# Storing rounded weight quarters at once, moving the GpSimd sums behind the last weight piece, reordering a piece's rounding steps, and turning one attention tile on TensorE

## The chip, the cores and the metric

The kernel runs on one core of a Trainium2 chip. The metric is device time in microseconds (us) of one execution, lower is better. A core has TensorE (PE, matrix products), VectorE (DVE), ScalarE (ACT) and GpSimd (POOL), and a queue on SyncE (SP) that here issues nearly all DMA transfers. [...]

## The reference

A local attention is followed by a Fourier mix and a two-layer network with a ReLU:

```python
q_c = q.reshape(B, H, nc, chunk, D)            # B=8, H=8, S=576, D=64, chunk=64
scores = 1/sqrt(D) * matmul(q_c, k_c.transpose)
attn = softmax(scores)                         # within each chunk of 64 tokens
x = matmul(attn, v_c)  -> (8, 576, 512)
u = x + real(fft(fft(x, axis=1), axis=2))
un = (u - mean) / sqrt(var + 1e-6)             # over the 512 features
out = u + maximum(un @ w_ch1, 0) @ w_ch2       # w_ch1 512 x 2048, w_ch2 2048 x 512
```

q, k, v are float32. The two weight matrices arrive as float64, so the kernel rounds them to float32 itself, with integer operations on the two 32-bit words of each number.

## The kernel before

**Groups and steps.** Tokens are cut into tiles of 128 rows, three kinds of them: LO and HI (low and mirrored high chunks of one batch) and RE (the middle chunks of two batches). For each of the eight batches there is a group of four tiles (LO and HI), and a ninth group holds the four RE tiles. The main loop runs the network (`mlp`, L1234) group after group. Each `yield` of it is one step `t`. Group 0 has 16 steps up (`up_first`, L1044, one weight piece each) and 16 steps down (`down_plain`, L1088, one row block `m` of `w_ch2` each); a step is eight matmul records of 128x512 here[...]. From group 1 on the down product, and from group 2 on the up product, use a Strassen-Winograd form with seven products in place of eight (`up_halves` L1124, `down_halves` L1168). It needs sums of weight quarters; these are computed once, put into HBM (`s1`, `s2`) and fetched again as slabs.

**What is interleaved.** While group g is multiplied, the attention and the Fourier mix of batch g+1 run as a generator (`side`, L1289), a due share per step. Attention of a tile has four parts: `att_T` turns q and k, `att_S` scores (tile `sc`), `att_P` turns the exponentials, `att_V` multiplies by v (tile `xp`). From the third batch on (`n >= first[2]`) `att_T` is a DVE block transpose (L366) on a special load layout (L203, 8 DMAs for q and 8 for k); before that it is four PE transposes each and an ACT copy (L374 to L387). The third batch begins with tile 9, an RE tile, and its `att_T` falls into step 15 of group 0. The Fourier mix (`fourier`, L742) is: products into `z` (L669), ACT copies (L694, L708), three DVE operations (`z_joined`, L696), ACT copies into `zr` and `zf`, products into `mix` (L788), sums, mean and variance, then normalising (`normed` L929) and turning (`turned` L947) into the next group's `unT`.

**Rounding the weights.** There are 32 pieces of 128x512: 16 of `w_ch1`, then 16 of `w_ch2`, landing in seven raw buffers: two in `yall`, five in `xall`. Pieces from `N_LAST` = 26 on use three of the buffers only. `round_weight(i)` (L301) does the head of piece i and the tail of piece i-1: DVE masks the fraction (L322) and the exponent (L325), ACT converts the fraction (L314) and the exponent in two steps (L317, L320); then DVE adds the low word (L335), merges the sign (L336) and multiplies (L337). L336 is the last to read the raw buffer, after which the next piece is loaded (L299). `round_next` is called once or twice a step, except in a step where `side` reports a heavy part.

**Sums for the second matrix.** `keep2(i)` (L1006), i = 0 to 3, makes four sums on GpSimd (L1017) from quarters of `w2`, in `yall` for even i and in `xall` for odd i, and then queues seven stores on SP: three plain quarters and four sums (L1021). The loop takes five parts of it as soon as more than 26 pieces have been begun, the rest behind the last piece. `keep1` (L989) does the like for the first matrix in group 1, and uses `yall` for even i.

**ReLU.** At steps 4, 8, 12 and 16, ACT applies the ReLU to four PSUM tiles (L1065), which frees those PSUM buffers for PE's next products. In ACT's order these come behind the three ACT parts of the piece that was begun in the step before.

Of the kernel before, what the change touches and what calls it, by code (L numbers as in the profile page):

```python
# [8 lines left out]
FP32 = mybir.dt.float32  # L9
U32 = mybir.dt.uint32  # L10
# [6 lines left out]
def kernel(  # L17
# [32 lines left out]
    nc = tc.nc  # L50
# [130 lines left out]
    def load(n, which="qk"):  # L181

        for src, dst, nm, eng in ((q, qs, "q", nc.sync), (k, ks, "k", nc.scalar if n == 0 else nc.sync)):
            if nm not in which:
                continue
            if n == first[1] and nm == "q":
                one_p.tile([128, 96], FP32, tag="pad_c", name="pad_c")  # L190
            if n < first[1]:
                i = 2 * n + (nm == "k")
                t = start[:, (4 + i) * DM:(5 + i) * DM].rearrange("p (j r d) -> p j (r d)", r=2, d=D)
            else:
                t = one_p.tile([128, NJ, 4 * D], FP32, tag=nm, name=nm)
            if n >= first[2]:
                (b0, c0), (b1, c1) = chunks(n)
                parts = [(0, 32, b0, min(c0, c1))] if b0 == b1 else [(0, 16, b0, c0), (16, 16, b1, c1)]
                for g in range(4):
                    e, x0 = g // 2, g % 2 * 32  # L200
                    for r0, rows, b, c in parts:
                        from_ = src[b, e:H:2, c * CH:c * CH + 4 * rows, :].rearrange("j (p t) d -> p j (t d)", t=4)
                        eng.dma_start(  # L203
                            out=t[32 * g + r0:32 * g + r0 + rows, :, 0:4 * D - 32],
                            in_=from_[:, :, x0:x0 + 4 * D - 32],
                        )
                dst[n] = t
                continue
            t = t.rearrange("p j (r d) -> p (j r) d", d=D)[:, 0:H]
            (b0, c0), (b1, c1) = chunks(n)  # L210
            if b0 == b1 and c1 == c0 + 1:
                parts = [(0, 128, b0, c0)]
            else:
                parts = [(0, CH, b0, c0), (CH, CH, b1, c1)]
            for p0, np_, b, c in parts:
                eng.dma_start(
                    out=t[p0:p0 + np_], in_=src[b, :, c * CH:c * CH + np_, :].rearrange("h p d -> p h d")
                )
            dst[n] = t
# [70 lines left out]
    def raw(i):  # L290
        return spaces[raws[i]].bitcast(U32).rearrange("p (f r) -> p f r", r=2)
# [9 lines left out]
    def round_weight(i, later=None, parts="ht"):  # L301

        if "h" in parts and i < len(pieces):
            w, t = pieces[i][0], raw(i)
            lo, hi, wi = t[:, :, 0], t[:, :, 1], w.bitcast(U32)  # L310
            p = power[i] = three_p.tile([128, 512], U32, tag="o", name="power")

            def fraction(w=w, wi=wi):
                nc.scalar.activation(out=w, in_=wi, func=ACTF.Copy, scale=2.0 ** -20, bias=1.0)  # L314

            def exponent(p=p):
                nc.scalar.activation(out=p, in_=p, func=ACTF.Relu, scale=-1.0, bias=top[:, 0:1])  # L317

            def power_(p=p):
                nc.scalar.activation(out=p, in_=p, func=ACTF.Relu, scale=-8.0, bias=top[:, 1:2])  # L320

            nc.vector.tensor_scalar(wi, hi, 0x000FFFFF, None, ALU.bitwise_and)  # L322
            if later is None:
                fraction()
            nc.vector.tensor_scalar(p, hi, 0x7FF00000, None, ALU.bitwise_and)  # L325
            if later is None:
                exponent()
                power_()
            else:
                later += [fraction, exponent, power_]  # L330
        if "t" in parts and 0 < i <= len(pieces):
            w, t = pieces[i - 1][0], raw(i - 1)
            lo, hi = t[:, :, 0], t[:, :, 1]
            p = power.pop(i - 1)
            nc.vector.scalar_tensor_tensor(w, lo, 2.0 ** -52, w, ALU.mult, ALU.add)  # L335
            nc.vector.scalar_tensor_tensor(p, hi, 0x80000000, p, ALU.bitwise_and, ALU.bitwise_or)  # L336
            nc.vector.tensor_tensor(out=w, in0=w, in1=p.bitcast(FP32), op=ALU.mult)  # L337
            r = raws.pop(i - 1)
            if i - 1 + len(spaces) < N_EARLY or r < N_LATE:
                free.append(r)  # L340
            load_weight(max(raws, default=i - 1) + 1)
# [9 lines left out]
    def att_T(n, which="qk"):  # L351

        if n >= first[2]:
            for src, dst, nm in ((qs, qT, "qT"), (ks, kT, "kT")):
                if nm[0] not in which:
                    continue
                a = src.pop(n).rearrange("p j (t b d) -> p j t b d", t=4, b=2)[:, :, :, 0]  # L360
                t = one_p.tile([128, NJ, 2, CH + 1], FP32, tag=nm, name=nm)
                low = kind(n) == LO and nm == "qT"
                to = t[:, :, :, CH:0:-1] if low else t[:, :, :, 0:CH]
                if kind(n) == HI:
                    to = to[:, :, ::-1]
                nc.vector.transpose(out=to.rearrange("p j c (r t) -> p j t c r", t=4), in_=a)  # L366
                if low:
                    nc.gpsimd.tensor_copy(t[:, :, :, 0:1], t[:, :, :, CH:CH + 1])
                dst[n] = t.rearrange("p j c t -> p (j c) t")
            if n + 1 < NT:  # L370
                load(n + 1, which)
            return
        a = qs.pop(n)
        pt = turn(lambda j: a[:, 2 * j:2 * j + 2, :].rearrange("p h d -> p (h d)"))  # L374
        t = one_p.tile([128, 2 * NJ, CH + 1], FP32, tag="qT", name="qT")
        low = kind(n) == LO
        nc.scalar.copy(t[:, :, CH:0:-1] if low else t[:, :, 0:CH], pt.rearrange("p j (c t) -> p (j c) t", c=2))
        if low and n < first[1]:
            nc.scalar.copy(t[:, :, 0:1], t[:, :, CH:CH + 1])
        elif low:  # L380
# [625 lines left out]
    def keep2(i):  # L1006

        m = 2 * i
        b11, b12 = w2[:, m:m + 2, 0:HM], w2[:, m:m + 2, HM:DM]
        b21, b22 = w2[:, HF + m:HF + m + 2, 0:HM], w2[:, HF + m:HF + m + 2, HM:DM]  # L1010
        to = xall[:, 2 * G:2 * G + 4, 0:DM] if i % 2 else yall
        o1, o2, o3, o4 = (to[:, j].rearrange("p (m e) -> p m e", m=2) for j in range(4))
        for out_, in0, in1, op in (
            (o1, b12, b11, ALU.subtract), (o2, b22, o1, ALU.subtract),
            (o3, b22, b12, ALU.subtract), (o4, b21, o2, ALU.subtract),
        ):
            nc.gpsimd.tensor_tensor(out=out_, in0=in0, in1=in1, op=op)  # L1017
            yield
        to = s2.rearrange("o p (m e) -> o p m e", m=HF)
        for o, a in enumerate((b11, o2, o1, o3, b21, b22, o4)):  # L1020
            nc.sync.dma_start(out=to[o, :, m:m + 2], in_=a)  # L1021
        yield

    first_of = {1: 2, 2: 1}
    n_slab = {1: 0, 2: 0}
# [214 lines left out]
    with tc.manual_schedule():  # L1240
# [61 lines left out]
        for g in range(NG):  # L1302
            begin.append(begin[-1] + (KF if g < first_of[1] else 2 * HF) + (KF if g < first_of[2] else 2 * NO))
        ready_at = [begin[g] + (2 * KF - 7 if g < first_of[2] else 2 * HF + 4) for g in range(NG)]
        conv2 = iter([step for i in range(HF // 2) for step in [keep2(i)]])
        conv1 = iter([step for i in range(4) for step in [keep1(i)]])

        def chain(gens):
            for gen in gens:
                yield from gen  # L1310

        n_sum = 0
        conv2, conv1 = chain(conv2), chain(conv1)
        t = 0
        for g in range(NG):
            for _ in mlp(g):
                t += 1
                heavy = False
                if t == 8:
                    nc.scalar.copy(tk, early_tk[:, :, :, 0:NE])  # L1320
                if cur < len(sides):
# [8 lines left out]
                            pass  # L1330
                        cur, done = cur + 1, 0
                if not heavy:
                    round_next()
                    if t <= 2 or t < KF and t % 4 == 0 or t >= KF + 3:
                        round_next()

                for _ in range(3):
                    if n_w > len(pieces) or n_w > N_LAST and n_sum < 5:
                        next(conv2, None)
                        n_sum += 1  # L1340
                if t == begin[1] - 1:
                    for _ in conv2:
                        pass
# [58 lines left out]
```

## Time and profile before

| what | value |
|---|---|
| runs before | 1083.34, 1083.85, 1084.11 us (median 1083.85) |
| the profiled execution's own time | 1083.94 us |
| its span, first to last instruction | 1082.2 us |
| PE busy | 1057.6 us, 98% |
| DVE, ACT, POOL busy | 586.8, 309.4, 328.6 us |
| moved by DMA | 192.65 MB |
| mean granted TensorE clock | 0.995 |

The span is told from its start. Group 0 goes up from about 50 to 115 us and down from 117 to 195 us; group 1 follows. A "wait" line names the engine, the tile that it was about to write, and the instruction whose end released it. A timeline line has the start, the duration, engine, line, operation, output<-inputs and shape; an idle time before it stands in square brackets.

### The profile page before, as it was taken

The numbers are of one execution on the slowest core, as the hardware profiler recorded it, in microseconds if no ns is written. First come the engines' busy times: TensorE is split into PE (matmuls) and PEld (weight loads), VectorE is DVE, ScalarE is ACT, GpSimd is POOL, SyncE is SP. The second block draws the span as 40 slices with busy tenths as digits, with TensorE's granted clock in tenths as the row PEclk, the third lists the DMA queues.
The fourth block names the chain that finished last, engine by engine and source line by source line (L and its number), as shares of the span: only waits on it lengthen the run. The fifth ranks groups of instructions, "written<-read, shape, count | busy, mean of one in ns | idle before, by whom it ended". The sixth has DMA issues, their size and how long they took to land.

```text
span 1082.2 us, 19747 instructions
## 1 busy us (share of the span) xinstructions
PE 1057.6 (98%) x7410; PEld 841.1 (78%) x7410; DVE 586.8 (54%) x1271; ACT 309.4 (29%) x730; POOL 328.6 (30%) x475
## 2 busy tenths in 40 slices
PE   8999989999999999999999999999999999999998
PEld 6645445446888888788888888888888888888887
DVE  4899986325556555664555555735664534323411
ACT  4788463222113320232122311331134103101300
POOL 4301026384513350163215331525151401310140
PEclk9999989999999999999999999999999999999999
DMA  8766555598557635793578356854663355346232
GB/s 176 237 196 180 153 175 199 143 292 275 192 172 229 198 118 173 222 266 105 168 214 252 112 176 179 253 174 150 184 199 104 144 173 177 123 151 213 78 117 78
DMA packets 147948, 192.65 MB, mean 178 GB/s; under 512 B 66284, under 2 KB 104172, under 8 KB 140686
## 3 DMA queue, kind: packets, MB, share of 16 engines
q1 hardware_dynamic: 144204, 187.98, 57.1%
q10 hardware_dynamic: 3330, 2.76, 1.0%
q8 instruction: 59, 0.97, 0.3%
q0 software_dynamic: 320, 0.66, 0.3%
q14 instruction: 35, 0.29, 0.1%
HBM read 167.22 MB, written 24.12 MB: 177 GB/s over the span
## 4 chain that ended last, share of the span: by engine, by line
PE 81%; DVE 6%; DMA 6%; ACT 4%; SPq 2%; issue 1%; POOL 1%; DVEq 0%; ACTq 0%; POOLq 0%
PE pb L1190 21%; PE pa L1141 17%; PE pa L1190 15%; PE pb L1141 13%; PE pt L347 3%; PE up L1074 2%; PE dn L1095 2%; PE mix L788 2%; PE z L669 1%; PE sc L398 1%; PE xp L448 1%; PE up L1054 1%; DMA v<-in_v_dram 1%; DMA out_dram<-o 1%; DMA q<-in_q_dram 1%
## 5 line engine op out<-in xcount | busy, mean ns | idle before, releaser
L1141 PE MATMUL pa<-unT,wa 128*128 128x256 f32 x672 | 159.9, 381 | 2.5 <-DVE wa L1149 2.5
L1141 PEld LDWEIGHTS pa<-unT,wa 128*128 128x128 f32 x672 | 126.3, 190 | 20.3 <-DVE wa L1149 3.0
L1042 POOL TENSOR_TENSOR h<-h 128x256 f32<-128x256 f32 x64 | 55.2, 870 | 232.6 <-DVE wb L1040 140.1
L1190 PE MATMUL pa<-wb,h 128*128 128x256 f32 x512 | 115.7, 380 | 0.0
L1190 PE MATMUL pb<-wb,h 128*128 128x256 f32 x512 | 114.9, 379 | 0.0
L1141 PE MATMUL pb<-wa 128*128 128x256 f32 x448 | 106.6, 381 | 0.0
L1190 PEld LDWEIGHTS pa<-wb,h 128*128 128x128 f32 x512 | 96.1, 190 | 12.9
L1190 PEld LDWEIGHTS pb<-wb,h 128*128 128x128 f32 x512 | 96.3, 190 | 12.6
L1141 PEld LDWEIGHTS pb<-wa 128*128 128x128 f32 x448 | 84.3, 190 | 11.5
L1095 PE MATMUL dn<-wb,h 128*128 128x512 f32 x128 | 60.8, 625 | 2.6 <-ACT h L1065 2.6
L505 POOL COPY xall<-xall 1x512 f32<-1x512 f32 x28 | 17.3, 617 | 149.7 <-DVE xall L465 120.4
L1147 DVE TENSOR_TENSOR wa<-pb,wa 128x256 f32<-128x256 f32 x56 | 23.8, 424 | 69.7 <-ACT wa L1146 69.7
L1190 PE MATMUL pb<-wb,yall 128*128 128x256 f32 x256 | 58.2, 381 | 0.0
L1190 PE MATMUL pb<-wb 128*128 128x256 f32 x256 | 57.7, 379 | 0.0
L1190 PE MATMUL pa<-wb,yall 128*128 128x256 f32 x256 | 57.6, 379 | 0.0
L1074 PE MATMUL up<-unT,wa 128*128 128x512 f32 x128 | 56.8, 596 | 0.0
L1146 ACT COPY wa<-pa 128x256 f32<-128x256 f32 x56 | 20.8, 372 | 123.8 <-PE pa L1141 81.0
L1141 PE MATMUL pa<-wa 128*128 128x256 f32 x224 | 53.9, 383 | 0.0
L1141 PE MATMUL pb<-unT,wa 128*128 128x256 f32 x224 | 53.0, 380 | 0.0
L1190 PEld LDWEIGHTS pa<-wb,yall 128*128 128x128 f32 x256 | 48.0, 190 | 6.1
L1190 PEld LDWEIGHTS pb<-wb,yall 128*128 128x128 f32 x256 | 47.7, 190 | 6.3
L1190 PEld LDWEIGHTS pb<-wb 128*128 128x128 f32 x256 | 47.7, 190 | 5.9
(265 smaller groups left out, 1770.0 us busy)
## 6 DMA issues: line engine op xcount, KB each, us to landing
wb<-s SPq DMA_DIRECT2D x56, 1024.0 KB
wa<-s SPq DMA_DIRECT2D x196, 256.0 KB
xall<-in_moe_w_ch_dram SPq DMA_DIRECT2D x22, 512.0 KB
q<-in_q_dram SPq DMA_DIRECT2D x96, 112.0 KB
k<-in_k_dram SPq DMA_DIRECT2D x96, 112.0 KB
v<-in_v_dram SPq DMA_DIRECT2D x124, 64.0 KB
yall<-in_moe_w_ch_dram SPq DMA_DIRECT2D x10, 512.0 KB
s<-wb SPq DMA_DIRECT2D x20, 256.0 KB
```

What stands on the lines that cost most here:

```text
L347: nc.tensor.transpose(pt[:, j, :], src(j), ident)
L398: nc.tensor.matmul(out=sc[t0:t0 + CH, e, j * CH:(j + 1) * CH], lhsT=a[r0:r0 + D, 2 * j + c, 0:CH], rhs=b[r0:r0 + D, 2 * j + c, 0:CH], star ...
L448: nc.tensor.matmul(out=xp[0][e][t0:t0 + CH, j * DV:(j + 1) * DV], lhsT=a[r0:r0 + CH, j, t0:t0 + CH], rhs=b[r0:r0 + CH, c, j, :], start=Tru ...
L505: nc.gpsimd.tensor_copy(to, from_)
L788: nc.tensor.matmul(out=mix[:, cols], lhsT=zt[:, T], rhs=tab, start=(T == 0), stop=(T == 3), skip_group_check=True,)
L1042: nc.gpsimd.tensor_tensor(out=h1[:, m, hi], in0=h1[:, m, lo], in1=h1[:, m, hi], op=ALU.subtract)
L1074: nc.tensor.matmul(out=up, lhsT=w1[:, kk, m * 128:(m + 1) * 128], rhs=unT[:, kk], start=(kk == 0), stop=(kk == KD - 1),)
L1095: nc.tensor.matmul(out=dn, lhsT=h1[:, m, s * 128:(s + 1) * 128], rhs=w2[:, m, :], start=(m == 0), stop=(m == KF - 1),)
L1141: nc.tensor.matmul(out=dst, lhsT=w[:, kk, r], rhs=rhs[o][:, kk], start=(o in (0, 1) and kk == 0), stop=(kk == 1), skip_group_check=True,)
L1146: nc.scalar.copy(a, dst)
L1147: nc.vector.tensor_tensor(out=b, in0=pbs[r][:, 0], in1=a, op=ALU.add)
L1190: nc.tensor.matmul(out=dst, lhsT=lhs[:, m], rhs=w[:, m], start=(o in (0, 2) and m == 0), stop=(m == HF - 1), skip_group_check=True,)
```

## The change

Four things are altered.

1. `keep2` stores only its four sums. A new `keep2_whole(i)` queues the three plain quarters of `w2` as soon as the pieces that they consist of have been begun and left behind by two more. The sums are all taken behind the last piece, in the order i = 1, 0, 3, 2.
2. In `round_weight` the exponent mask comes first, then two of the three tail operations of the piece before, then the fraction mask, then the tail's product. ACT gets exponent, second exponent step, fraction.
3. In steps 3, 7, 11 and 15 the three ACT parts of the piece are held back (`late`) until the next step's products and ReLUs have been issued.
4. The bounds `n >= first[2]` in `load` and `att_T` become `n > first[2]`: tile 9 is loaded in natural order (two DMAs for q, two for k) and turned by PE and ACT.

```diff
@@ load, att_T
-            if n >= first[2]:
+            if n > first[2]:
@@ round_weight
-        if "h" in parts and i < len(pieces):
+        head, tail = "h" in parts and i < len(pieces), "t" in parts and 0 < i <= len(pieces)
+        if head:
...
-            nc.vector.tensor_scalar(wi, hi, 0x000FFFFF, None, ALU.bitwise_and)
-            if later is None:
-                fraction()
             nc.vector.tensor_scalar(p, hi, 0x7FF00000, None, ALU.bitwise_and)
             if later is None:
                 exponent()
                 power_()
+        if tail:
+            w_, t_ = pieces[i - 1][0], raw(i - 1)
+            p_ = power.pop(i - 1)
+            nc.vector.scalar_tensor_tensor(w_, t_[:, :, 0], 2.0 ** -52, w_, ALU.mult, ALU.add)
+            nc.vector.scalar_tensor_tensor(p_, t_[:, :, 1], 0x80000000, p_, ALU.bitwise_and, ALU.bitwise_or)
+        if head:
+            nc.vector.tensor_scalar(wi, hi, 0x000FFFFF, None, ALU.bitwise_and)
+            if later is None:
+                fraction()
             else:
                 later += [fraction, exponent, power_]
-        if "t" in parts and 0 < i <= len(pieces):
...
-            nc.vector.scalar_tensor_tensor(w, lo, 2.0 ** -52, w, ALU.mult, ALU.add)
-            nc.vector.scalar_tensor_tensor(p, hi, 0x80000000, p, ALU.bitwise_and, ALU.bitwise_or)
-            nc.vector.tensor_tensor(out=w, in0=w, in1=p.bitcast(FP32), op=ALU.mult)
+        if tail:
+            nc.vector.tensor_tensor(out=w_, in0=w_, in1=p_.bitcast(FP32), op=ALU.mult)
@@ keep2
-        for o, a in enumerate((b11, o2, o1, o3, b21, b22, o4)):
+        for o, a in ((1, o2), (2, o1), (3, o3), (6, o4)):
             nc.sync.dma_start(out=to[o, :, m:m + 2], in_=a)
         yield
+
+    def keep2_whole(i):
+        m = 2 * i
+        to = s2.rearrange("o p (m e) -> o p m e", m=HF)
+        for o, m0, e0 in ((0, m, 0), (4, HF + m, 0), (5, HF + m, HM)):
+            nc.sync.dma_start(out=to[o, :, m:m + 2], in_=w2[:, m0:m0 + 2, e0:e0 + HM])
@@ main loop
-        conv2 = iter([step for i in range(HF // 2) for step in [keep2(i)]])
+        conv2 = iter([step for i in range(HF // 2) for step in [keep2(i ^ 1)]])
...
             for _ in mlp(g):
                 t += 1
                 heavy = False
+                for do in late:
+                    do()
+                late = []
...
                 if not heavy:
-                    round_next()
+                    round_next(late if t < KF and t % 4 == 3 else None)
...
-                for _ in range(3):
-                    if n_w > len(pieces) or n_w > N_LAST and n_sum < 5:
+                while n_whole < HF // 2 and n_w > KF + HF + 2 * n_whole + 2:
+                    keep2_whole(n_whole)
+                    n_whole += 1
+                if n_w > len(pieces):
+                    for _ in range(3):
                         next(conv2, None)
-                        n_sum += 1
```

More of the change, by code (lines that the diff above doesn't have):

```diff
@@ L301, in round_weight @@
     def round_weight(i, later=None, parts="ht"):
-        if "h" in parts and i < len(pieces):
+        head, tail = "h" in parts and i < len(pieces), "t" in parts and 0 < i <= len(pieces)
+        if head:
             w, t = pieces[i][0], raw(i)
-            lo, hi, wi = t[:, :, 0], t[:, :, 1], w.bitcast(U32)
+            hi, wi = t[:, :, 1], w.bitcast(U32)
             p = power[i] = three_p.tile([128, 512], U32, tag="o", name="power")
@@ L328, in round_weight @@
                 power_()
+        if tail:
[7 more added lines that the diff above has]
+                fraction()
             else:
                 later += [fraction, exponent, power_]
-        if "t" in parts and 0 < i <= len(pieces):
[L332 to L337, printed above, removed]
+        if tail:
+            nc.vector.tensor_tensor(out=w_, in0=w_, in1=p_.bitcast(FP32), op=ALU.mult)
             r = raws.pop(i - 1)
@@ L351, in att_T @@
     def att_T(n, which="qk"):
-        if n >= first[2]:
+        if n > first[2]:
             for src, dst, nm in ((qs, qT, "qT"), (ks, kT, "kT")):
@@ L1310, in chain @@
                 yield from gen
-        n_sum = 0
+        n_whole, late = 0, []
         conv2, conv1 = chain(conv2), chain(conv1)
```

## The prediction

> **What bounds the kernel now.** I read the page first, then PE's waits, then the granted clock in short windows, and then the timelines of DVE, ACT, SP and POOL around each wait.
>
> ```profile
> PE 1057.6 (98%) x7410; PEld 841.1 (78%) x7410; DVE 586.8 (54%) x1271; ACT 309.4 (29%) x730; POOL 328.6 (30%) x475
> ...
> PE mix L788 <- ACT zr L735: 4.4, 1, 4.4
> PE dn L1095 <- ACT h L1065: 2.6, 1, 2.6
> PE pt L347 <- ACT un L942: 2.1, 3, 1.0
> PE sc L398 <- DVE rd L461: 1.4, 1, 1.4
> PE up L1054 <- ACT h L1065: 1.1, 2, 0.6
> ```
>
> PE sets the time. Only what PE loses can be won, and in the waits that is little: the five lines shown are 11.6 us, and all but 1.6 us of them (two of the `un` waits at 44 us) lie between 64 and 217 us, where the weights are rounded. From 262 us on PE waits 2.5 us in all, and the change does not touch that part. Behind the two longest waits the clock drops too:
>
> ```profile
> 117.00:119.00 2.00, 1.81 (x2) 0.84 (x3) 1.57 (x3) 1.59 (x4) 0.22 (x2) 0.55 1.04 236
> 156.00:158.00 2.00, 1.83 (x6) 1.70 (x7) 1.97 (x5) 1.97 (x9) 0.00 (x0) 0.50 1.06 388
> ```
>
> (Columns: window, length, busy PE, PEld, DVE, ACT, POOL, clock, DMA share, GB/s.) The first down step takes 5.39 us instead of 3.60; after the second wait the `mix` products and a step lose 2.7 us. So the most that can be won is about 0.64 + 0.44 (up) + 2.57 + 1.8 (seam from up to down) + 4.42 + 2.7 (mix) + 0.5 + 1.4 = 14.5 us.
>
> Why is `mix` late? ACT's copies before it stand behind the rounding of piece 29, and DVE is late with that:
>
> ```profile
> 139.61 0.69 DVE L337 TENSOR_TENSOR wb<-wb,power 128x512 f32<-128x512 f32 x1
> 140.66 1.33 DVE L322 TENSOR_SCALAR wb<-xall 128x512 uint32<-128x512 uint32 x1 [0.36 <-DMA xall<-in_moe_w_ch_dram]
> 141.91 1.49 DVE L325 TENSOR_SCALAR power<-xall 128x512 uint32<-128x512 uint32 x1
> 143.33 1.75 DVE L335 SCALAR_TENSOR_TENSOR wb<-xall,wb 128x512 f32<-128x512 uint32 x1
> 145.01 0.68 DVE L336 SCALAR_TENSOR_TENSOR power<-xall,power 128x512 uint32<-128x512 uint32 x1
> ...
> 140.44 1.26 POOL L1017 TENSOR_TENSOR yall<-wb,yall 128x512 f32<-128x512 f32 x1 [10.62 <-DVE wb L337]
> 141.67 1.45 POOL L1017 TENSOR_TENSOR yall<-wb 128x512 f32<-128x512 f32 x1
> 143.08 1.45 POOL L1017 TENSOR_TENSOR yall<-wb,yall 128x512 f32<-128x512 f32 x1
> ```
>
> The three DVE operations beside the three sums take 4.57 us; elsewhere 0.42 + 0.42 + 0.68 = 1.52. The sums cost DVE 3.05 us here, and the first sum, at 128.56, stretches L520 from 0.69 to 1.77: 1.08 more.
>
> **What the Trainium skill says.** "SBUF — State Buffer", section "SBUF: two separate sides": VectorE and GpSimd share one port pair, held as an exclusive lock for a whole instruction. The trace agrees: each of those DVE operations is longer by about one sum. "TensorE: Matmul & The Clock Gate", section "The HAM clock gate": a free-running window of 3413 ns, half clock after an idle one. The records show half clock for 3.41 us from 117.2 and 6.83 us from 154.8, behind idle times of 2.57 and 4.42 us, and none behind 1.43 us. [...]here a 512 KB piece issued at 137.00 ends a wait at 140.66, 3.6 us.
>
> **The change part by part.** The profiled execution's span is 1082.2 of its own 1083.94 us, so 1.7 us lie outside; its time is 0.1 above the median. I subtract from the median.
>
> *Held-back ACT parts.* At steps 4 and 12 the ReLUs no longer wait for 1.9 us of rounding on ACT: 0.64 + 0.44 = 1.08 won. Hidden cost: the piece's ACT parts come after four ReLUs (2.0 us), and DVE's next piece waits for them.
>
> *New step order.* DVE keeps five operations, 2.60 us a piece (heads at 132.41, 135.02, 137.62). But the fraction leaves DVE at 0.34 + 0.60 + 0.60 + 0.34 = 1.88 and ACT at 2.5 us into a piece, and is needed at 2.94; before, the most urgent ACT result had 1.5 us of slack. Wherever ACT has the q and k copies (0.95) or ReLUs in between, DVE waits. Going through the ACT queue from 47 to 112 us I find waits of 0.7 at the start, and about 1.3 (step 4), 1.0 (step 8) and 1.6 (step 12), part of it caught up where DVE waited for PE before (0.83 at 79.8); two old waits of 0.67 go. I take DVE as 2.0 us later at 112 us; bounds 0 and 3.5. This is covered while DVE leads PE: at 90.8 it begins piece 16, which PE needs at 117.
>
> *Tile 9 on PE.* DVE loses two transposes (1.09 + 1.08, at 112.34 and 113.28): 2.2 won, which offsets the 2.0. PE gains eight transposes, 0.87 us by the other tiles' records; ACT two copies, 0.95. Of SP's 16 DMAs (97.1 to 106.0) four remain; q and k should land near 103, and PE needs them at about 109. The second transpose needs the PSUM buffer that ACT's copy of the exponentials frees, now behind a fraction: 0.5 wait. The ReLUs stand behind the two copies: 0.3.
>
> *Seam.* Last `xp` ends at 114.62; minus 1.08, plus 0.87, 0.5, 0.3 gives the first down product at 115.2 instead of 117.19: 2.0 won, and with no half clock 1.8 more. PE is 3.8 earlier.
>
> *Sums moved.* DVE reaches L470 1.3 earlier (it no longer waits 1.14 for PE), L520 takes 0.69 (2.4), the pieces 24 to 29 run free of sums and of the 0.59 of load waits: 3.6 more, 6.0 in all. Against this stand the early stores: three of 256 KB go into the DMA engines beside the load of piece 29. A load now has 0.34 + 0.69 + 2.60 = 3.63 us before its use, and takes 3.5 to 3.6 alone; I take 1.0 us of delay (bounds 0 and 3). So piece 29 is through 5.0 earlier, ACT's copies follow, and `mix` begins at 151.2 instead of 156.2. PE, ready at 148, waits 3.2 there.
>
> *What is late next.* From `mix` to the normalised tile (`un`, ready at 177.4) runs a chain ACT, DVE, GpSimd, DVE, ACT of 21 us in which PE is not a link: two pieces on ACT, `y`, the sums, statistics. PE's own work there is 18.1 us at full clock. So whatever PE would win behind `mix` (the 2.7) is lost in front of `un`, where its wait grows from 0.5 to about 3. The fraction's new place costs this chain 0.3. Won at `un`: 4.7 to 5.7, I take 5.2.
>
> *Sums behind it.* GpSimd idles from 186.0 to 191.4 (only a 0.1 us memset); four more sums (4 x 1.27 = 5.1) fill this. Queued behind them: `keep1`'s sums, which also wait for the last `yall` stores, some 4 us later than now; their own stores follow the k load of tile 12 on SP (211 us), so it is hidden. On SP the nine plain stores of i = 1 to 3 leave the stretch 168 to 188. Tile 12's k load, for which DVE waits 8.65 us and PE then 1.43 at 217, comes behind fewer stores but beside 1 MB of late ones: between 1.4 won and 2 lost; I take 0.3 won.
>
> Sum: 5.2 + 0.3 = 5.5 us. 1083.85 - 5.5 = 1078.3.
>
> **Rivals.**
>
> *A, everything falls into place.* No load delay, DVE without new waits, and the chain to `un` shortens with it: `mix` is then bound by PE's own `z` products (148.05 - 3.8, plus the 8.1 from there to `mix`, less the 3.6 that ACT was behind), at 148.8, 7.4 won; with the 1.4 at 217 and 0.5 at `un`, 8 to 10: 1074 to 1076. For it: DVE's gains are measured. Against: the chain behind `mix`.
>
> *B, the stores take the place of the sums.* With three raw buffers a load slowed to 5 or 6 us holds DVE in each of pieces 27 to 29; 2 to 3.5 us of the 6.0 are lost: 1080 to 1082. For it: the DMA engines are at 0.92 to 1.06 from 110 to 122 us and in bursts later. Against: from 122 to 138 they are below 0.2.
>
> *C, slower.* Third-batch loads behind the sums: SP works in order, and the last four sum stores stand before q of tile 12, the output stores and k. If k of tile 12 lands over 6 us later in relation to PE than now, PE's wait at 217 grows from 1.4 to over 7 and eats all: 1084 to 1087. For it: that wait exists already. Against: SP now spends 6.3 us (190.75 to 197.06) at the v loads that stand before these stores, and GpSimd ends about when it did.
>
> *D, the held-back parts do nothing*, since DVE's slip undoes them and `un` stays where it is: 1083 to 1085.
>
> **How the numbers follow.** Forecast (1076.5 to 1080) 0.52, A 0.13, B 0.22, C 0.08, D 0.05. Two executions differ by 0.07%; I call 0.2% (2.2 us, 1081.7) about what can be told from no change. B lies below it in 0.15 of its 0.22, D is split with most of it as same. Faster 0.80, same 0.12, slower 0.08. Leaving out C and half of A gives 1075.0 to 1082.0. The forecast's own range is 1076.5 to 1080; half a window of half clock at the `un` wait (1.7 us) lies within it.
>
> **What would show it.** Right: no PE wait of `up` or `dn` for a ReLU; no half clock near 117; no DVE operation of a piece over 0.9 us between 120 and 150; a `mix` wait of 2 to 3.5; a wait for `un` of 2 to 3.5; GpSimd busy without a break up to `keep1`. Wrong: DVE waiting for weight loads over 2 us in pieces 27 to 29 (B), PE waiting over 4 us for a score of tile 12 (C), or a PE wait in the up steps for a DVE product of a piece, which the 2.0 us slip takes as impossible.

## Result, and the profile after

The changed kernel takes 1076.57 us (median of 4 runs, 1075.50 to 1076.94); the kernel before, run beside it, 1083.98 us (1083.34 to 1086.40). The ratio is 0.9927, with a 95% interval of 0.9913 to 0.9942: faster by 7.4 us, where 5.5 were forecast. The median lies at the lower edge of the forecast range (1076.5 to 1080); two of the four executions, 1076.41 and 1075.50, lie below it. The profiled execution took 1076.41 us with a span of 1074.6, against 1083.94 and 1082.2 before, so the spans differ by 7.6.

First the page of the changed kernel (busy time, share of the span, instructions):

```profile
PE 1054.5 (98%) x7418; PEld 840.0 (78%) x7418; DVE 578.6 (54%) x1269; ACT 311.6 (29%) x732; POOL 330.2 (31%) x475
```

PE has eight instructions more (the turning of tile 9) and yet is busy 3.1 us less, since in this execution none of its work runs at half clock any more. The waits of PE (total, times, longest):

```profile
PE pt L350 <- ACT un L945: 3.0, 3, 1.4
...
PE mix L791 <- DVE y L802: 2.1, 1, 2.1
PE mix L791 <- ACT zr L738: 1.7, 1, 1.7
PE pa L1151 <- DVE wa L1159: 1.6, 2, 1.3
...
PE sc L401 <- DVE rd L464: 1.0, 2, 0.6
```

No wait for a ReLU is left, neither at `up` nor at `dn`. The wait for `zr` fell from 4.4 to 1.7. A wait that did not exist before stands behind it, in front of the third group of `mix` products: 2.1 us for `y`. The same two stretches as before (window, length, busy PE, PEld, DVE, ACT, POOL, clock, DMA share, GB/s):

```profile
117.00:119.00 2.00, 2.00 (x7) 0.82 (x6) 1.55 (x5) 1.38 (x3) 0.22 (x2) 1.00 1.15 229
156.00:158.00 2.00, 0.06 (x1) 0.09 (x1) 1.93 (x4) 0.33 (x3) 1.92 (x2) 1.00 0.00 0
```

The clock is 1.00 in both. In the second PE does nothing: that is the new wait. Up to the last microsecond the record of the clock shows 0.5 for 10.2 us before and for none after. That holds for the profiled execution: the four executions of the changed kernel have mean clocks of 1.000, 1.000, 0.998 and 0.999, so two of them had some half clock too.

Where PE stands, in its timeline (start, duration, what it runs; idle time before it and its releaser in brackets):

```profile
115.35 2.84 PE L1105 MATMUL dn<-wb,h 128*128 128x512 f32 x6
...
149.97 0.49 PE L791 MATMUL mix<-ce,zr 128*128 128x129 f32 x2 [1.74 <-ACT zr L738]
157.94 0.46 PE L791 MATMUL mix<-ce,zf 128*128 128x129 f32 x2 [2.07 <-DVE y L802]
171.82 0.66 PE L350 MATMUL pt<-ident,un 128*128 128x128 f32 x4 [1.41 <-ACT un L945]
...
210.25 0.69 PE L401 MATMUL sc<-kT,qT 64*64 64x64 f32 x32 [0.31 <-DVE rd L464]
```

| point | before | after | earlier by | forecast |
|---|---|---|---|---|
| first down product | 117.19 | 115.35 | 1.8 | 2.0 |
| end of the first down step | 122.58 | 119.05 | 3.5 | 3.8 |
| first `mix` product | 156.17 | 149.97 | 6.2 | 5.0 |
| turning of `un` | 177.45 | 171.82 | 5.6 | 5.2 |
| score of tile 12 | 217.01 | 210.25 | 6.8 | 5.5 |
| span | 1082.2 | 1074.6 | 7.6 | 5.5 |

At the two points of the seam and at `un` the forecast holds within 0.4 us; at `mix` it was 1.2 too low. The rest came behind `un`: 1.1 at the score of tile 12, whose wait fell from 1.43 to 0.31, and 1.0 at `pa` in groups 3 and 5, where the waits fell from 1.77 to 1.28 and from 0.77 to 0.27; half a microsecond was lost between them, at a new wait of 0.65 for the next score, at 226.59. (The profiled execution after began group 0's up products of 128x512 0.54 us later than the one before, 51.49 against 50.95, so told from there each lead is half a microsecond larger.)

Last the rounding of the pieces near 140 us on DVE, in the timeline:

```profile
138.59 0.68 DVE L339 TENSOR_TENSOR wb<-wb,power 128x512 f32<-128x512 f32 x1
140.38 0.43 DVE L323 TENSOR_SCALAR power<-xall 128x512 uint32<-128x512 uint32 x1 [1.10 <-DMA xall<-in_moe_w_ch_dram]
140.72 0.69 DVE L330 SCALAR_TENSOR_TENSOR wb<-xall,wb 128x512 f32<-128x512 uint32 x1
141.32 0.70 DVE L331 SCALAR_TENSOR_TENSOR power<-xall,power 128x512 uint32<-128x512 uint32 x1
141.93 0.43 DVE L333 TENSOR_SCALAR wb<-xall 128x512 uint32<-128x512 uint32 x1
```

The stretched operations (1.33, 1.49, 1.75 before) are gone; the wait of 1.10 us in front of this piece is new (before, two waits for loads in this stretch were 0.36 and 0.23).

The sums did not leave DVE alone altogether. The first late sum falls beside the last product of piece 30, in the chain to `y`:

```profile
153.71 0.69 DVE L330 SCALAR_TENSOR_TENSOR wb<-xall,wb 128x512 f32<-128x512 uint32 x1 [2.23 <-ACT wb L315]
...
155.25 1.76 DVE L339 TENSOR_TENSOR wb<-wb,power 128x512 f32<-128x512 f32 x1
156.94 0.41 DVE L801 TENSOR_TENSOR y<-y,mix 128x255 f32<-128x255 f32 x1
...
155.08 1.38 POOL L1020 TENSOR_TENSOR xall<-wb 128x512 f32<-128x512 f32 x1 [28.69 <-DMA s<-wb]
```

L339 takes 1.76 us instead of 0.68. ACT's copy for `y` had ended at 156.32, so about 0.6 us of the new wait of 2.07 comes from this sum; most of the rest comes from the wait of 2.23 for a fraction.

### The profile page after: what moved, and what is told of

It reads as the page before. It is cut to its first block, busy times and chain, and to the rows that moved or that the text cites. A ratio compares the mean times of both kernels' runs of the same rounds, so it can differ in the third digit from the quotient of the medians.

```text
span 1074.6 us, 19747 instructions
## 1 busy us (share of the span) xinstructions
PE 1054.5 (98%) x7418; PEld 840.0 (78%) x7418; DVE 578.6 (54%) x1269; ACT 311.6 (29%) x732; POOL 330.2 (31%) x475
## 4 chain that ended last, share of the span: by engine, by line
PE 78%; DMA 6%; DVE 4%; POOL 3%; ACT 3%; SPq 3%; issue 2%; POOLq 0%; DVEq 0%; ACTq 0%
PE pb L1200 21%; PE pa L1151 17%; PE pa L1200 16%; PE pb L1151 12%; PE up L1084 2%; PE pt L350 2%; PE up L1064 2%; DMA xall<-in_moe_w_ch_dram 2%; PE mix L791 2%; PE z L672 1%; DMA v<-in_v_dram 1%; PE xp L451 1%; SPq L216 1%; DMA q<-in_q_dram 1%; PE sc L401 1%
## 5 line engine op out<-in xcount | busy, mean ns | idle before, releaser
L1200 PEld LDWEIGHTS pb<-wb,h 128*128 128x128 f32 x512 | 96.3, 190 | 12.6
L1105 PE MATMUL dn<-wb,h 128*128 128x512 f32 x128 | 57.5, 597 | 0.0
```

The costliest lines, as they stand in the source:

```text
L1105: nc.tensor.matmul(out=dn, lhsT=h1[:, m, s * 128:(s + 1) * 128], rhs=w2[:, m, :], start=(m == 0), stop=(m == KF - 1),)
L1200: nc.tensor.matmul(out=dst, lhsT=lhs[:, m], rhs=w[:, m], start=(o in (0, 2) and m == 0), stop=(m == HF - 1), skip_group_check=True,)
```

## The experiments

The theory: the sums on GpSimd cost DVE about 4 us before `mix`, the seam gave PE its lead there, and from `mix` to `un` a chain through ACT, DVE and GpSimd decides. The rivals: that storing the quarters early, not the place of the sums, is what wins; or that one of the smaller edits carries it.

### Each part undone

*Sums and stores as before.* `keep2` stores all seven parts, its first five steps run from piece 27 on.

```diff
-        for o, a in ((1, o2), (2, o1), (3, o3), (6, o4)):
+        for o, a in enumerate((b11, o2, o1, o3, b21, b22, o4)):
...
-                if n_w > len(pieces):
-                    for _ in range(3):
+                for _ in range(3):
+                    if n_w > len(pieces) or n_w > N_LAST and n_sum < 5:
...
```

(`keep2_whole` goes, and the sums are taken in the order i = 0 to 3 again)

> The changed kernel with the sums and stores of the second matrix as before (five parts of the first sum early, all seven stores behind the sums). Theory 1 (the time is set by the chain VectorE, ScalarE, GpSimd into mix and on to the normalised tile, so what shortens VectorE's way there counts): the three sums run beside VectorE again and cost it 3 to 4 us, less the 1.1 us wait for a load that the early stores bring; mix begins 2.5 to 3 us later and the run is at 1079 to 1080. Theory 2 (the gain is made on TensorE at the seam from up to down and by the half clock that does not come there): 1076.5 to 1077.5.

Measured: 1081.61 us, ratio to the kernel before 0.9983 (0.9973 to 0.9994). PE waits 4.50 us for `mix`, which begins at 155.07, 5.1 later than in the changed kernel, and the clock is at half for 6.8 us. That is more than the 2.5 to 3 us and 1079 to 1080 of the theory, on its side of the rival.

*The old order of a piece's operations.*

```diff
+            nc.vector.tensor_scalar(wi, hi, 0x000FFFFF, None, ALU.bitwise_and)
+            if later is None:
+                fraction()
             nc.vector.tensor_scalar(p, hi, 0x7FF00000, None, ALU.bitwise_and)
...
-        if head:
-            nc.vector.tensor_scalar(wi, hi, 0x000FFFFF, None, ALU.bitwise_and)
...
```

(the two tail operations go back ahead of the product alone, behind both masks)

> The changed kernel with the steps of a piece in the old order. Theory 1: VectorE's piece takes 2.60 instead of 2.48 us, 0.7 us over the six pieces before mix, but the waits for a fraction (0.9, 0.8, 0.9, 0.4 us before 105 us) go; the chain behind mix wins 0.3. Net within 0.8 us of the changed kernel, 1075.8 to 1077.4. Theory 2: the order has nothing to do with the seam, 1076.6.

Measured: 1076.18 us (6 executions), ratio 0.9924 (0.9905 to 0.9944): no different from the changed kernel. The wait for `y` is absent, the other two are longer:

```profile
149.07 0.80 PE L788 MATMUL mix<-ce,zr 128*128 128x129 f32 x2 [2.56 <-ACT zr L735]
170.36 0.65 PE L347 MATMUL pt<-ident,un 128*128 128x128 f32 x4 [1.56 <-ACT un L942]
```

Half clock for 3.4 us begins at 148.97, behind the longer wait, and still the time is the same. So the reordering itself won nothing that can be told. It brought shorter pieces (2.48 us instead of 2.60) and new waits for the fraction; that these two cancel fits, but was not tried.

*No ACT parts held back.*

```diff
-                    round_next(late if t < KF and t % 4 == 3 else None)
+                    round_next()
```

> The changed kernel without holding back the ScalarE parts of the pieces of steps 3, 7, 11 and 15. Theory 1: TensorE waits for ReLUs again in the up steps and at the seam, some 1.5 to 2.5 us, but it waits 1.7 and 2.1 us at mix for a chain that is not touched, so most of this is absorbed: 1076.3 to 1077.6. Theory 2: the seam decides and the half clock comes back: 1078.5 to 1080.5.

Measured: 1080.64 us, ratio 0.9962 (0.9951 to 0.9973). The theory (1076.3 to 1077.6) fell: the loss is not absorbed. PE waits for ReLUs again, at `up` longer than it did in the kernel before (1.1), probably because the fraction that stands before those ReLUs on ACT is now masked later (DVE waits 2.09 us for one at 69.22):

```profile
PE up L1064 <- ACT h L1075: 2.0, 3, 1.2
...
PE dn L1105 <- ACT h L1075: 1.0, 1, 1.0
```

And the chain to `mix` is touched, which the theory denied. DVE's pieces begin 1.5 us later from 130 us on (130.65 instead of 129.12), and then it waits longer for a load:

```profile
145.81 0.44 DVE L323 TENSOR_SCALAR power<-xall 128x512 uint32<-128x512 uint32 x1 [2.23 <-DMA xall<-in_moe_w_ch_dram]
```

`mix` begins at 152.93, 3.0 us later than in the changed kernel, with the same two waits (1.87 and 2.05) and 3.4 us of half clock behind the second, at 162.04. Holding the parts back is thus worth more on DVE's way to `mix` than in PE's own waits for ReLUs.

*Tile 9 turned by DVE again.*

```diff
-            if n > first[2]:
+            if n >= first[2]:
```

(in `load` and `att_T`)

> The changed kernel with the first tile of the third batch turned by VectorE again. Theory 1: VectorE is 2.2 us later from 113 us on and does not wait for TensorE before mix, so mix and the normalised tile are 2 us later although TensorE has 0.9 us less to do: 1078 to 1079. Theory 2: TensorE's 0.9 us less counts, 1075.7 to 1076.6.

Measured: 1080.08 us, ratio 0.9964 (0.9953 to 0.9975). PE is ready for `mix` at 146.6 instead of 148.2 and waits 5.41 us, since DVE joins `z` at 149.07 instead of 147.04, about what the two transposes take that it has again (2.2 us). The record shows 6.8 us of half clock from 151.17. The median is 1.1 above the expected range.

Undone singly, sums and stores cost 5.0 us, the held-back parts 4.1, the turning 3.5, by the medians. That is 12.6 for a change worth 7.4: each undoing reopens or lengthens pauses of PE, and a pause can bring half clock with it. Half clock is seen in all three profiles, for 6.8, 3.4 and 6.8 us. How much of each loss it is stays open: in the kernel with the old order 3.4 us of it cost nothing that can be told.

*The first edit alone*, in the kernel before: sums behind the last piece, quarters stored early, nothing else.

> The kernel before with the first edit alone: plain quarters stored early, sums behind the last piece. No change at the seam from up to down, where PE still waits 2.6 us at half clock. Theory (the parts meet in the same places): PE has no lead at the mix, so the mix wait of 4.4 and the half clock behind it go and VectorE is not asked for more; 1078 to 1080, that is 4 to 6 us won of the 7.4, and the other three edits alone are worth 2 to 3. Rival (the first edit needs the earlier seam): less than 3 us won, 1081 or more. Rival (the first edit is all of it): 1077 or less.

Measured: 1079.70 us, ratio 0.9965 (0.9955 to 0.9976), in the range of the theory, and the half clock behind `mix` is gone. The first edit alone wins about 3.8 us by its ratio, the other three alone (the first run above) about 1.8, all together 7.9: about 2 us more come from having both, hardly more than these intervals leave open.

### Which half of the first edit?

*Sums early, quarters early.*

```diff
-                if n_w > len(pieces):
-                    for _ in range(3):
-                        next(conv2, None)
+                for _ in range(3):
+                    if n_w > len(pieces) or n_w > N_LAST and n_sum < 5:
+                        next(conv2, None)
+                        n_sum += 1
...
```

(the order of the sums, too, is i = 0 to 3 again)

> The changed kernel, but with the first set of GpSimd sums taken as soon as more than 26 pieces are begun, as before; the plain quarters are still stored early and apart. Theory (contention on VectorE): three sums again lie beside piece operations near 140 us and lengthen them by 3 us together, one more lengthens a row operation by 1.1, so the mix wait of PE grows from 1.7 to about 4.5 us and the time to 1080 to 1082. Rival (the stores of the sums, queued ahead of weight loads, were the cost): piece operations of 1.3 to 1.8 us are seen but the mix wait stays at about 2 and the time at 1076 to 1077.

Measured: 1080.25 us, ratio 0.9963 (0.9953 to 0.9974). The stretched operations are back, in DVE's timeline, beside three sums (POOL at 138.07, 139.29 and 140.70):

```profile
126.59 1.76 DVE L523 TENSOR_TENSOR sum<-xall 128x512 f32<-128x512 f32 x1 [0.29 <-POOL sum L522]
...
138.07 1.54 DVE L323 TENSOR_SCALAR power<-xall 128x512 uint32<-128x512 uint32 x1 [0.15 <-DMA xall<-in_moe_w_ch_dram]
139.54 1.76 DVE L330 SCALAR_TENSOR_TENSOR wb<-xall,wb 128x512 f32<-128x512 uint32 x1
141.22 1.75 DVE L331 SCALAR_TENSOR_TENSOR power<-xall,power 128x512 uint32<-128x512 uint32 x1
```

They take 1.54 + 1.76 + 1.75 = 5.05 us instead of 0.43 + 0.69 + 0.70 = 1.82: 3.2 lost, and 1.07 at L523. The `mix` wait is 5.78 and `mix` starts at 154.97, 5.0 later. With the quarters stored early, the place of the sums is worth some 4 us (1080.25 against 1076.57).

*Sums late, all seven stores behind them.*

```diff
-        for o, a in ((1, o2), (2, o1), (3, o3), (6, o4)):
+        for o, a in enumerate((b11, o2, o1, o3, b21, b22, o4)):
...
-                while n_whole < HF // 2 and n_w > KF + HF + 2 * n_whole + 2:
-                    keep2_whole(n_whole)
-                    n_whole += 1
```

> The changed kernel, but all seven stores of a set wait for its sums, so that none is issued before the last piece. Theory (contention): no loss, 1075.5 to 1077; the wait of 1.1 us for the load of a piece at 140 us goes, the mix wait is 1.7 or less, and at most 0.5 us come back at the score of tile 12, whose k load stands behind more stores. Rival (storing the quarters early is what won): 1079 or more, with a longer PE wait for the score of tile 12 or for the slabs of group 1.

Measured: 1084.38 us, ratio 1.0007 (0.9993 to 1.0021). Here the theory fell: the whole gain is gone. In PE's timeline everything is as in the changed kernel up to `un`, and then it stands:

```profile
150.14 0.49 PE L791 MATMUL mix<-ce,zr 128*128 128x129 f32 x2 [1.42 <-ACT zr L738]
158.11 0.46 PE L791 MATMUL mix<-ce,zf 128*128 128x129 f32 x2 [2.07 <-DVE y L802]
171.99 0.66 PE L350 MATMUL pt<-ident,un 128*128 128x128 f32 x4 [1.41 <-ACT un L945]
...
216.87 1.14 PE L401 MATMUL sc<-kT,qT 64*64 64x64 f32 x32 [6.76 <-DVE rd L464]
```

PE waits 6.76 us for the score of tile 12, because DVE waits 13.42 us for k of that tile, and half clock follows (6.8 us). This is rival C of the prediction, in a kernel that has all of the change but the early stores. So the two halves of the first edit cannot be valued apart. With the other three edits in place the medians are:

| | quarters stored with their sums | quarters stored early |
|---|---|---|
| first sums early | 1081.61 | 1080.25 |
| all sums late | 1084.38 | 1076.57 |

Late sums alone lose 2.8 us, early stores alone win 1.4, both together win 5.0.

The load wait of 1.10 us near 140 us has two sources. Without early stores DVE waits 0.17 + 0.68 = 0.85 us for loads of pieces there in this kernel and 0.43 in the one with four sums a step (below); with early stores and the pieces in the same steps it waits 1.10 (changed kernel), 1.63 (old order), 2.41 (no parts held back) and 1.98 (tile 9 on DVE).

### Why k of tile 12 is late

In the traces each of these transfers has one of eight semaphores (101 and 103 to 109, counted 0 to 7 here), in turn in the program's order, whether SP or ACT issues it. Each issue waits on its own semaphore first, that is, until the transfer before it on that semaphore has landed. The Trainium skill, "DMA: Bandwidth & Descriptors", section "Anatomy of one DMA" (written for transfers that GpSimd issues), says that DMA engines never wait on a semaphore, the issuing sequencer does; the trace agrees for SP, which takes 6.98 us over four issues for v below instead of 2.65. In that order lie four output stores of group 0 that ACT issues, which cannot start before the last down products are added. Whatever is eight places behind one of them is held until it has landed, and all that stands behind it on SP too.

In the changed kernel k of tile 11 has semaphores 0 to 3 and v 4 to 7, and the output stores come next, on 0, 2, 5 and 7, mixed with the last four sums on 1, 3, 4 and 6; the first transfer to be held is q of tile 12. In the kernel with late stores the output stores stand among k of tile 11 and v; the fourth v transfer is held, with seven stores and then q and k of tile 12 behind it. SP's timeline, of the changed kernel:

```profile
183.02 2.65 SPq L226 DMA_DIRECT2D v<-in_v_dram  x4
185.76 2.02 SPq L1024 DMA_DIRECT2D s<-yall  x4
190.91 1.76 SPq L203 DMA_DIRECT2D q<-in_q_dram  x4
...
200.45 2.03 SPq L203 DMA_DIRECT2D k<-in_k_dram  x4
```

and of the kernel with late stores:

```profile
185.15 6.98 SPq L226 DMA_DIRECT2D v<-in_v_dram  x4
192.19 0.60 SPq L1024 DMA_DIRECT2D s<-wb  x1
192.88 1.41 SPq L1024 DMA_DIRECT2D s<-yall  x3
...
196.26 2.13 SPq L203 DMA_DIRECT2D q<-in_q_dram  x4
...
206.09 4.01 SPq L203 DMA_DIRECT2D k<-in_k_dram  x4
```

In all these kernels PE comes to the score of tile 12 a fixed 22.4 us after DVE's first output row of group 0 (217.01 - 1.43 - 193.15 before, 210.25 - 0.31 - 187.51 after, 216.87 - 6.76 - 187.68 here). So what counts is when DVE begins to transpose k, told from that same row; PE waits for what exceeds 21.3:

| kernel | k transposed, us after the first output row | PE's wait, us |
|---|---|---|
| before | 22.7 | 1.43 |
| changed | 21.6 | 0.31 |
| first edit alone | 22.8 | 1.54 |
| stores late | 28.1 | 6.76 |
| stores late, four parts a step | 25.6 | 4.28 |
| pieces 30, 31 later | 28.1 | 6.77 |
| the same, old order | 27.9 | 6.57 |
| the same, output stores by GpSimd | 24.1 | 2.81 |

The lower rows are of the runs that follow. *Stores late, sums four a step:*

```diff
-                    for _ in range(3):
+                    for _ in range(4):
                         next(conv2, None)
```

> As the kernel that stores all seven parts of a set behind its sums, but with four parts of the sums per step instead of three, so that the last seven stores come before the v load on SP and not behind it. The same stores, sums and bytes, in another place of the order. Theory (each transfer on SP waits for the one eight before it in the program's order, the output stores that ScalarE issues at the end of group 0 are among these, and whatever comes behind them in the order is held until they have landed): only the v load is still held, q of tile 12 is issued 3.5 to 5 us after the first output row instead of 8.6, k follows, PE's wait for the score of tile 12 falls from 6.8 to 2 to 3.5 us and the time from 1084.4 to 1079 to 1081. Rival (the bytes of the late stores hold k back): the wait stays above 5.5 us and the time above 1083.

Measured: 1084.80 us, ratio 1.0013 (1.0003 to 1.0024). Half a hit: the seven stores now precede v, q of tile 12 is issued 6.7 us after the first output row instead of 8.6, and the wait falls by 2.5, but to 4.28 and not under 3.5. The time did not follow. The first output row itself is 2.0 us later (189.66), with 3.4 us of half clock at 160 us before it, so PE comes to the end of that wait only 0.5 us earlier (216.37), and the `pa` waits are 2.3 us instead of 1.1.

*Pieces 30 and 31 one step later*, behind the first `y`, to test the chain behind `mix`:

```diff
-                if not heavy:
+                if not heavy and t != 23:
```

> The changed kernel, but the two pieces that were begun between the z copies and the first y (pieces 30 and 31) are begun one step later, behind the first y. Theory (behind the mix it is the chain through ScalarE, VectorE and GpSimd that sets when un is ready, and the two pieces stand in it): PE's second mix wait, 2.07 us for y, goes or falls under 0.5, the un wait falls to 0.7 or less, and the time falls by 1.5 to 3 us to 1073.5 to 1075. Rival (PE's own work between mix and un and the three statistics set it): the waits change place, for example to a row block of the down products that waits for piece 30 or 31, and the time stays at 1076 to 1077.

Measured: 1084.38 us, ratio 1.0002 (0.9990 to 1.0014). PE's timeline:

```profile
150.31 0.49 PE L791 MATMUL mix<-ce,zr 128*128 128x129 f32 x2 [1.58 <-ACT zr L738]
170.52 0.80 PE L350 MATMUL pt<-ident,un 128*128 128x128 f32 x4 [2.09 <-ACT un L945]
181.72 0.62 PE L451 MATMUL xp<-v,pT 64*64 64x65 f32 x26 [0.41 <-ACT unT L960]
217.11 1.13 PE L401 MATMUL sc<-kT,qT 64*64 64x64 f32 x32 [6.77 <-DVE rd L464]
```

The theory fell. The wait for `y` is gone and `un` comes 1.3 us earlier, so the two pieces did stand in the chain. But the wait for `un` grew to 2.09 rather than falling, 3.4 us of half clock follow it (from `un` to `xp` 11.2 us instead of 9.5), and in the order of the transfers v and q of tile 12 came behind the held ones, and the last four sum stores between q and k: 6.5 us more of waiting at the score of tile 12. So 1.3 were won and more was lost at two places.

*The same with the old order of a piece's operations:*

> As the kernel with pieces 30 and 31 one step later, and with the old order of the five VectorE operations of a piece. Theory: VectorE no longer stands 2.2 us for a fraction near 154 us, and the early y makes that of no account, so the time is within 0.5 us of the same kernel with the new order, 1073.5 to 1075. Rival (the new order is needed for VectorE to be early enough): 1 to 2 us longer than the new order, with a mix wait over 2.5 us.

Measured: 1082.19 us, ratio 0.9981 (0.9970 to 0.9993). Not the 1073.5 to 1075 expected: the same wait at tile 12. PE reaches `un` at 167.83, the earliest of all runs.

*Pieces 30 and 31 later, q and k of tile 12 through GpSimd's queue:*

```diff
             if nm not in which:
                 continue
+            if n == 12:
+                eng = nc.gpsimd
```

> As the kernel with pieces 30 and 31 one step later, but q and k of tile 12 are loaded through GpSimd's queue and so stand behind no store on SP. Theory (that kernel won 1.3 us up to un and lost all of it and more at the score of tile 12, whose loads were held on SP): PE's wait for the score of tile 12 falls from 6.8 us to 2 or less, and the time from 1084.4 to 1075 to 1078. Rival (the late sums on GpSimd hold the loads in the same way): the wait stays over 4 us, time over 1080.

Measured: 1080.26 us, ratio 0.9972 (0.9962 to 0.9982). The wait at the score of tile 12 is 1.27, as expected; the time is not. A second wait of 2.1 us for a later score, `pa` waits of 2.7 and half clock behind two pauses (3.4 us each time) take the rest.

*The output stores off the eight semaphores*, in the kernel with pieces 30 and 31 later and the old order: the four that ACT issues are issued by GpSimd, with all else left in place.

```diff
-                    eng = nc.scalar if r else nc.sync
+                    eng = (nc.gpsimd if n in groups[0] else nc.scalar) if r else nc.sync
```

> As the kernel with pieces 30 and 31 one step later and the old order of a piece's operations, but the four output stores of group 0 that ScalarE issues are issued by GpSimd, and so are no longer among the transfers that SP's issues wait for. Bytes and all other transfers are the same. Theory (the loads of tile 12 are late because issues on SP wait for transfers earlier in the program's order, and these stores, which cannot start before group 0 ends, stood in front of the v load and eight more transfers): SP's wait of 6.6 us at the v load goes, k of tile 12 is transposed 21 to 24 us after the first output row instead of 27.9, PE's wait for the score of tile 12 falls from 6.6 to under 1.5 us and the time from 1082.2 to 1075 to 1077.5. Rival (the bytes of the late stores, or GpSimd behind its sums, hold the loads): the wait stays over 4 us and the time over 1080.

Measured: 1077.08 us (6 executions), ratio 0.9938 (0.9919 to 0.9956), against 1082.19 without it. SP's longest waits from 150 to 225 us without the edit hold this line,

```profile
SPq L226 <- DMA out_dram<-o: 6.2, 2, 5.4
```

and with it no wait at L226 for an output store. Its timeline then shows the v load issued in one go, with q right behind it:

```profile
183.72 2.65 SPq L226 DMA_DIRECT2D v<-in_v_dram  x4
186.46 2.73 SPq L203 DMA_DIRECT2D q<-in_q_dram  x4
189.29 2.44 SPq L1021 DMA_DIRECT2D s<-yall  x4
```

PE's wait fell from 6.57 to 2.81 us, not under the 1.5 expected, since k is transposed 24.1 us after the row, at the end of the range of 21 to 24: it is still behind four sum stores and eight output stores. The bytes are the same and the time fell by about 5 us, so it is the waiting of issues for output stores, not the volume of the late stores, that holds the loads. No version beat the changed kernel by more than can be told; the one with the old order ties with it.

## Why the prediction was right

The sign and the path came out as worked out, and the time just within its range; sizes were off in both directions and partly offset each other. At `mix` PE was 1.2 us further ahead than forecast, and the wait for `y`, which was not forecast, then took 2.07; that `un` came within 0.4 is in part luck. Three of the signs that were named did not come as named: the `mix` waits are 1.74 and 2.07 instead of one of 2 to 3.5, the wait for `un` is 1.41 and not 2 to 3.5, and GpSimd stands still for 3.47 us before the first sum of `keep1` (189.42), until stores from `yall` have landed. The 0.07% between executions came from three runs; beside the later ones the kernel before ranges from 1080.4 to 1088.8, 0.8%, so only the medians of many executions tell a difference of 2 us.

**Held-back ACT parts.** Right as to the waits: no `up` or `dn` wait for a ReLU is left, and undoing it brings 3 us of them. That DVE would reach `mix` later without it was not foreseen. Two small waits for scores, 0.39 and 0.48 us at 66.66 and 106.16, were not foreseen.

**Seam.** Right: 1.8 earlier at the first down product for 2.0, 3.5 for 3.8 at the end of its step, no half clock.

**New step order.** The slip of DVE at 112 us was put at 2.0 and is about 1.1. That a piece stays at 2.60 us was wrong: heads at 129.12, 131.60 and 134.08 are 2.48 apart, as the fraction mask fills the gap that stood between L336 and L337. The waits for the fraction were right in kind; the largest is not where I looked for it but at 153.71 (2.23 us), between the `z` copies and `y`, and there it makes most of the new `mix` wait.

**Sums moved.** Right: with the sums early the three operations are 3.2 us longer for the 3.05 counted, and the 1.08 at L520 is 1.07. The sums' hold on DVE was read as about one sum for each operation; it is 0.91 to 1.07 us beside sums of 1.26 to 1.45. One late sum still does it, at 155.25. The load delay of 1.0 was right in size (1.10), and in cause only in part: waits of 0.43 to 0.85 are there without early stores. `mix` came at 149.97 instead of 151.2, mainly, it seems, by the slip and the shorter pieces of the paragraph above.

**What is late next.** Right in substance: 5.2 forecast, 5.6 measured at `un`. The wait was put in front of `un` alone, about 3; it is 2.07 in front of the third group of `mix` products and 1.41 in front of `un`. That the pieces on ACT stand in this chain is shown by the kernel that begins them later.

**Sums behind it.** The step that was mis-sized. The release of nine stores from the stretch before tile 12 was put at 0.3, between 1.4 won and 2 lost. The wait fell by 1.1, and without the early stores it would have risen by 5.3 (6.76 against 1.43). I counted stores and bytes on SP; what decides is behind which transfers q and k stand when the output stores hold the issue. Rival C was therefore nearer than its 0.08: its place and nearly its price were right (over 7 named, 6.76 measured in the kernel with late stores), and the early stores are what keeps the changed kernel out of it.

**The 1.0 us at `pa`** in groups 3 and 5 was not forecast; the prediction held that nothing changes from 262 us on. These waits vary between 0.5 and 2.7 us over the kernels without a pattern that I can name, so their cause stays open.

## What to carry to other kernels

When a stall on the critical engine is removed, look for the next load that is released by the end of the same phase, and count in the program's order which transfers stand between that release and the load; the load's absolute time before did not tell it here. Undo each half of a two-part edit: here the half that looked like bookkeeping (storing early) decided whether the half that removed the contention won 3.7 us or lost 2.8. Keep arithmetic on GpSimd away from the stretch in which DVE is the link that others wait for, even when GpSimd would otherwise be idle.

## What the runs showed of the hardware

- Whether a pause of PE brings half clock depends on where it falls. The Trainium skill, "TensorE: Matmul & The Clock Gate", section "The HAM clock gate", names a window of about 3.4 us that runs free, and half clock after an idle one. The window agrees: within each of the 14 profiles all changes of the clock lie whole multiples of 3.413 us apart. That the window must be idle throughout does not. With each profile cut into these windows, PE went to half clock behind all 19 windows at full clock in which it had been idle for 2.00 us or more, and behind none of the others, 60 of which had 1.0 to 1.84 us of idle time. So the pause of 2.09 before `un` (pieces later) brought half clock, for it lies within one window. The pause of 2.07 in the changed kernel brought none, for a boundary at 156.30 us cuts it into 0.42 and 1.64.
- Half clock lasted one window (3.4 us) in 11 cases and two (6.8 us) in 8. It went on where PE was idle for 0.83 us or more of the first window at half clock, and ended where it was idle for 0.10 or less.
- The kernels spread differently from run to run: the kernel before 1080.4 to 1088.8 in 57 executions beside the first four runs, those with a part undone 5.0 to 5.6 us in 20 to 22 each, the changed kernel 1.4 in 4 and the one with the old order 1.5 us in 6. Pauses that fall now within a window and now across a boundary would do this, but it was not tried, and the one with the old order has a pause of 2.56 us and half clock in its profile.
- In a piece, a dependent 128x512 operation of DVE right behind its producer starts 0.72 us after it (L336 to L337 before), an independent one 0.60; with the fraction mask in between, the five operations take 2.48 instead of 2.60 us.
